# Start and seam of a fused gated mix of linear attention and a SwiGLU FFN: order of the first keys, of the loads, and of the small products

## The chip, the cores and the metric

The kernel runs on one core of one Trainium2 chip. The metric is the device time of one execution in microseconds (us); the time of the kernel before is the median of three runs. A profiled execution gives the trace from which all durations here are read. The engines are PE (TensorE, with PEld for its weight loads), DVE (VectorE), ACT (ScalarE), POOL (GpSimd) and SP (SyncE, which here only issues DMAs).

## The reference

The input x has 2048 tokens of 512 elements, bf16. Two branches read it and a gate per token mixes them:

```python
def reference(A_x, A_wqkv, A_wo, B_x, B_w1, B_w3, B_w2, gate_w):
    def _A_ref(x, wqkv, wo):                      # H = 32 heads of Dh = 16
        ...
        phi = lambda t: jnp.where(t > 0, t + 1, jnp.exp(t)) + 1e-6
        pq, pk = phi(q), phi(k)
        kv = jnp.einsum("bhsd,bhse->bhde", pk, v)
        z = jnp.einsum("bhsd->bhd", pk)
        num = jnp.einsum("bhqd,bhde->bhqe", pq, kv)
        den = jnp.einsum("bhqd,bhd->bhq", pq, z)[..., None] + 1e-6
        o = num / den
        return ... @ wo
    def _B_ref(x, w1, w3, w2):                    # F = 1376
        ...
        h = _silu(gate) * up
        return ...                                # h @ w2
    x = A_x
    g = _sigmoid((x * gate_w).sum(-1, keepdims=True))
    a = _A_ref(x, A_wqkv, A_wo)
    b = _B_ref(x, B_w1, B_w3, B_w2)
    return g * a + (1 - g) * b
```

The attention is linear: kv and z are sums over all tokens, so every token's key must be known before the first output can be formed. The kernel uses kv = pk' (x wv) = (pk' x) wv, so it first accumulates XP = x' pk over the tokens and multiplies by wv once at the end.

## The kernel before, in words

Tokens are cut into 16 tiles of 128 (t = 0 to 15), four tiles make a block of 512 (tb = 0 to 3). The 512 input elements are four chunks (kc, or dc) of 128, since a matmul contracts over 128 partitions. F is 10 chunks of 128 (fc) and a remainder of 96.

**Loads.** DMAs are issued from two queues, each in order: SP's (`dq`, L92) and ACT's. x is wanted twice: with tokens on the partitions (`x_sb`), and transposed (`xT`). For the first block PE transposes x from `x_sb`; for the other three blocks a transposing DMA writes `xT` (L98). ACT's queue issues the four chunks of wk (L95). SP's issues x tile 0, x tiles 1 to 3, then for each later block a transposing load and a plain load (L98, L102), and then wq, the remainder's columns and the gate vector (`wr_sb`), wv, w1, w3, wo, w2.

**Start.** Eight matmuls of zeros (`warm`, L148) and one for a block mask run first. Then comes the key phase: for each tile `emit_k` (L155) transposes x on PE for t under 4 (L160, ACT copies the result out, L164), does four k matmuls (L167), and `phi` (L132) turns k into pk: an exponential on ACT, two operations on DVE. POOL adds pk into `pks`, the sum for z. Two tiles later (`SKEW`) `emit_xp` (L177) adds x' pk to `XP_ps`, four matmuls into four PSUM banks held as one tile. The first two q tiles of block 0 lie between the last XP products, so that PE has work while pk is made. Then ACT and DVE copy XP out in four pieces (L339, L341).

**Seam.** `psO` and `psQ`, the PSUM pools of two banks each that come next, lie where XP_ps was. PE's order is: q tiles 2 and 3, z (`z_ps`, a matmul of ones with pks in float32, L349), the remainder of the FFN for block 0 (`emit_rem`: 96 columns of w1 and w3 and the gate vector), kvT (16 small matmuls of wv with XP_sb, L360, masked to the heads' diagonal blocks by DVE, L364), FFN chunk 0, and W = kvT wo (L371, copied by ACT). `emit_den` (POOL: pq times z, `qz`, L200; DVE: the sum over each head, L203) is emitted for all four tiles right behind the remainder, and `emit_norm` (L251) behind it: 1/den times exp of the gate, POOL's `pqn` (L265), and a transposing DMA from SP into `pqT` (L270).

**Steady part.** For each block: the FFN chunks (`emit_ffn`, L275: four gate and four up matmuls, tanh on ACT, L293, two DVE operations, `gs` L295 and `hT` L298), then for each of its four tiles the next block's q, half of its remainder, the output product `emit_out` (15 matmuls in one PSUM bank, scaled by ACT, stored by SP), and the next block's den; then the next block's norm.

**What sets the order.** PE's order is the order of the program text (`manual_schedule` for PE alone, L143). The order on ACT, DVE, POOL and SP is chosen by the tile framework's scheduler from the emission order and its own cost estimates; each engine then runs its list strictly in that order. [...]

Of the kernel before, what the change touches and what calls it, by code (L numbers as in the profile page):

```python
# [8 lines left out]
ACT = mybir.ActivationFunctionType  # L9
# [3 lines left out]
FP32 = mybir.dt.float32  # L13
BF16 = mybir.dt.bfloat16
# [3 lines left out]
def kernel(  # L18
# [12 lines left out]
    nc = tc.nc  # L31
    P = nc.NUM_PARTITIONS

    Bb, S, D = A_x.shape
# [3 lines left out]
    KC = D // P  # L38
    NT = S // P
# [51 lines left out]
    x_r = x2d.rearrange("(t p) d -> p t d", p=P)  # L91
    dq = nc.sync  # L92
    dq.dma_start(out=x_sb[:, 0:1, :], in_=x_r[:, 0:1, :])
    for kc in range(KC):
        nc.scalar.dma_start(out=wk_sb[:, kc, :], in_=wqkv_r[:, kc, D : 2 * D])  # L95
    dq.dma_start(out=x_sb[:, 1:TPB, :], in_=x_r[:, 1:TPB, :])
    for tb in range(1, NTB):
        dq.dma_start(  # L98
            out=xT[:, :, tb * TB : (tb + 1) * TB], in_=x2d[tb * TB : (tb + 1) * TB, :],
            transpose=True,  # L100
        )
        dq.dma_start(  # L102
            out=x_sb[:, tb * TPB : (tb + 1) * TPB, :], in_=x_r[:, tb * TPB : (tb + 1) * TPB, :]
        )
    dq.dma_start(out=wq_sb[:], in_=wqkv_r[:, :, 0:D])
    dq.dma_start(out=wr_sb[:, :, 0:FR], in_=w1_r[:, :, FM:F])
# [24 lines left out]

    def phi(dst, ps):  # L132
        e = work.tile([P, D], BF16, tag="phi_e", name="phi_e")
        nc.scalar.activation(out=e[:], in_=ps, func=ACT.Exp)  # L134
        em = work.tile([P, D], BF16, tag="phi_m", name="phi_m")
        nc.vector.tensor_scalar(  # L136
            out=em[:], in0=e[:], scalar1=1.0, scalar2=1e-6, op0=ALU.min, op1=ALU.add
        )
        nc.vector.scalar_tensor_tensor(  # L139
            out=dst, in0=ps, scalar=0.0, in1=em[:], op0=ALU.max, op1=ALU.add  # L140
        )

    ctx.enter_context(tc.manual_schedule(engines={ENG.PE}))  # L143


    warm = psM.tile([P, TB], FP32, tag="mm", name="warm")
    for i in range(8):
        nc.tensor.matmul(warm[:], lhsT=zeros[:, 0:P], rhs=zeros[:], start=True, stop=True)  # L148
    mask_ps = psM.tile([P, P], FP32, tag="mm", name="mask_ps")
    nc.tensor.matmul(mask_ps[:], lhsT=EhT[:], rhs=EhT[:], start=True, stop=True)  # L150
# [1 line left out]

    st = {}

    def emit_k(t):  # L155
        ts_tok = slice(t * P, (t + 1) * P)
        if t < TPB:
            xTp = psM.tile([P, KC, P], BF16, tag="mm", name="xTp")
            for kc in range(KC):
                nc.tensor.transpose(  # L160
                    out=xTp[:, kc, :], in_=x_sb[:, t, kc * P : (kc + 1) * P],
                    identity=ident[:],
                )
            nc.scalar.activation(out=xT[:, :, ts_tok], in_=xTp[:], func=ACT.Copy)  # L164
        k_ps = psM.tile([P, D], FP32, tag="mm", name="k_ps")
        for kc in range(KC):
            nc.tensor.matmul(  # L167
                k_ps[:], lhsT=xT[:, kc, ts_tok], rhs=wk_sb[:, kc, :],
                start=(kc == 0), stop=(kc == KC - 1),
            )  # L170
        phi(pk_sb[:, t, :], k_ps[:])
        if t == 0:
            nc.gpsimd.tensor_copy(pks[:], pk_sb[:, t, :])
        else:
            nc.gpsimd.tensor_add(pks[:], pks[:], pk_sb[:, t, :])  # L175

    def emit_xp(t, XP_ps):  # L177
        for dc in range(KC):
            nc.tensor.matmul(  # L179
                XP_ps[:, dc, :], lhsT=x_sb[:, t, dc * P : (dc + 1) * P], rhs=pk_sb[:, t, :],  # L180
                start=(t == 0), stop=(t == NT - 1),
            )

# [14 lines left out]
    def emit_den(tb, tt):  # L198
        qz = work.tile([P, D], FP32, tag="qz", name="qz")
        nc.gpsimd.tensor_tensor(  # L200
            out=qz[:], in0=st[tb, "pq"][:, tt, :], in1=z_sb[:], op=ALU.mult
        )
        nc.vector.tensor_reduce(  # L203
            out=st[tb, "den"][:, tt, :], in_=qz[:].rearrange("p (h d) -> p h d", d=Dh),
            axis=AX.X, op=ALU.add,
        )
# [44 lines left out]
    def emit_norm(tb):  # L251
        rden = blk.tile([P, TPB, H], FP32, tag="rden", name="rden")
        den = st[tb, "den"]
        nc.vector.tensor_scalar(
            out=rden[:], in0=den[:], scalar1=1e-6, scalar2=None, op0=ALU.add
        )
        nc.vector.reciprocal(out=rden[:], in_=rden[:])
        nc.vector.tensor_tensor(  # L258
            out=rden[:], in0=rden[:],
            in1=st[tb, "el"][:, :, None].to_broadcast([P, TPB, H]), op=ALU.mult,  # L260
        )
        pqT = blk.tile([P, KC, TB], BF16, tag="pqT", name="pqT")
        for tt in range(TPB):
            pqn = work.tile([P, D], BF16, tag="pqn", name="pqn")
            nc.gpsimd.tensor_tensor(  # L265
                out=pqn[:].rearrange("p (h d) -> p h d", d=Dh),
                in0=st[tb, "pq"][:, tt, :].rearrange("p (h d) -> p h d", d=Dh),
                in1=rden[:, tt, :, None].to_broadcast([P, H, Dh]), op=ALU.mult,
            )
            nc.sync.dma_start(  # L270
                out=pqT[:, :, tt * P : (tt + 1) * P], in_=pqn[:], transpose=True
            )
        st[tb, "pqT"] = pqT

    def emit_ffn(tb, fc):  # L275
        tok_sl = slice(tb * TB, (tb + 1) * TB)
        fsl = slice(fc * P, (fc + 1) * P)
        if fc == 0:
            st[tb, "hT"] = blk.tile([P, FC, TB], BF16, tag="hT", name="hT")
        gate_ps = psM.tile([P, TB], FP32, tag="mm", name="gate_ps")  # L280
        for kc in range(KC):
            nc.tensor.matmul(  # L282
                gate_ps[:], lhsT=w1_sb[:, kc, fsl], rhs=xT[:, kc, tok_sl],
                start=(kc == 0), stop=(kc == KC - 1),
            )
        up_ps = psM.tile([P, TB], FP32, tag="mm", name="up_ps")
        for kc in range(KC):
            nc.tensor.matmul(  # L288
                up_ps[:], lhsT=w3_sb[:, kc, fsl], rhs=xT[:, kc, tok_sl],
                start=(kc == 0), stop=(kc == KC - 1),  # L290
            )
        th = work.tile([P, TB], BF16, tag="th", name="th")
        nc.scalar.activation(out=th[:], in_=gate_ps[:], func=ACT.Tanh, scale=0.5)  # L293
        gs = work.tile([P, TB], BF16, tag="gs", name="gs")
        nc.vector.scalar_tensor_tensor(  # L295
            out=gs[:], in0=th[:], scalar=1.0, in1=gate_ps[:], op0=ALU.add, op1=ALU.mult
        )
        nc.vector.tensor_tensor(  # L298
            out=st[tb, "hT"][:, fc, :], in0=up_ps[:], in1=gs[:], op=ALU.mult
        )  # L300
# [22 lines left out]
        nc.sync.dma_start(out=out2d[t * P : (t + 1) * P, :], in_=o_out[:])  # L323


    SKEW = 2
    with tc.tile_pool(name="psX", bufs=1, space=bass.MemoryType.PSUM) as psX:
        XP_ps = psX.tile([P, KC, D], FP32, tag="XP", name="XP_ps")
        for t in range(NT):
            emit_k(t)  # L330
            if t >= SKEW:
                emit_xp(t - SKEW, XP_ps)
        emit_q(0, 0, psM, "mm")
        emit_xp(NT - 2, XP_ps)
        emit_q(0, 1, psM, "mm")
        emit_xp(NT - 1, XP_ps)
        for dc in range(KC):
            if dc % 2 == 0:
                nc.scalar.activation(out=XP_sb[:, dc, :], in_=XP_ps[:, dc, :], func=ACT.Copy)  # L339
            else:  # L340
                nc.vector.tensor_copy(out=XP_sb[:, dc, :], in_=XP_ps[:, dc, :])  # L341
# [7 lines left out]
    nc.tensor.matmul(z_ps[:], lhsT=ones_f[:], rhs=pks[:], start=True, stop=True)  # L349
    nc.scalar.activation(out=z_sb[:], in_=z_ps[:], func=ACT.Copy)  # L350
    emit_rem(0, 0, psM, "mm")
    emit_rem(0, 1, psM, "mm")
    for tt in range(TPB):
        emit_den(0, tt)
    emit_norm(0)
    kvT_ps = psQ.tile([P, KC, P], FP32, tag="q", name="kvT_ps")
    for c in range(KC):
        csl = slice(c * P, (c + 1) * P)
# [6 lines left out]
        out=kvT_sb[:], in0=kvT_ps[:],  # L365
        in1=blockmask[:, None, :].to_broadcast([P, KC, P]), op=ALU.mult,
    )
    emit_ffn(0, 0)
    for c in range(KC):
        W_ps = psQ.tile([P, D], FP32, tag="q", name="W_ps")  # L370
        nc.tensor.matmul(W_ps[:], lhsT=kvT_sb[:, c, :], rhs=wo_sb[:, c, :], start=True, stop=True)  # L371
        nc.scalar.activation(out=W_sb[:, c, :], in_=W_ps[:], func=ACT.Copy, scale=2.0)

    for tb in range(NTB):
        for fc in range(1 if tb == 0 else 0, FC):
# [42 lines left out]
```

## Time and profile before

| | |
|---|---|
| median of three runs | 202.17 us (200.95 to 202.47) |
| profiled execution | 200.74 us, of it span 199.0 us |
| mean granted PE clock in the profiled execution | 0.957 |
| busy: PE, DVE, ACT, POOL | 182.3, 119.9, 67.2, 59.2 us |
| matmuls of 512 columns, four of them, full clock | 0.86 us |
| HBM read, written | 8.42 MB, 2.10 MB |

Busy time of PE counts a matmul from its start to its end, and matmuls overlap; what matters is when each group starts. The chain of waits is followed back from the last instruction and shows, in order of time, which engine held the end at each point. The windows give the busy time of each engine, the granted clock and the DMA share in a stretch of time. In the timeline's rows the columns are the start, the length, the engine, the line, the operation, and in brackets the idle time before it with what ended it. A trailing q (SPq, ACTq) means the issue of a DMA, which occupies the queue but not the engine's arithmetic.

### The profile page before, as it was taken

What the parts mean: (1) busy time and instruction counts of PE and PEld (TensorE: products, weight loads), DVE (VectorE), ACT (ScalarE), POOL (GpSimd) and SP (SyncE); (2) the same over time, 40 slices, a digit from 0 to 9 for tenths busy, and PEclk for the clock granted to TensorE, in tenths of its full rate; (3) what the DMA queues carried; (4) which work ended last, traced back from release to release, by engine and by line L of the source; (5) the groups of instructions that cost most, each with busy time, mean ns of one, the idle gap of its engine ahead of it and who ended that gap; (6) DMA issues with size and microseconds to landing.
All of it is one profiled execution on the core that took longest, in us unless ns stands there. A gap on an engine that the chain in (4) does not pass through costs nothing.

```text
span 199.0 us, 2401 instructions
## 1 busy us (share of the span) xinstructions
PE 182.3 (92%) x846; PEld 84.2 (42%) x863; DVE 119.9 (60%) x202; ACT 67.2 (34%) x124; POOL 59.2 (30%) x67
## 2 busy tenths in 40 slices
PE   7268999996939999999999999999999999999993
PEld 2123444442603445454444545444454544444440
DVE  0023488788593778655888765578776567878000
ACT  2132333335433334332333433233333323332121
POOL 4014266751736200333540033354003235500000
PEclk9955999999975999999999999999999999999999
DMA  5999999100002300011040001013100101400011
GB/s 183 153 288 289 292 398 354 55 0 2 2 13 43 79 0 0 13 56 37 30 105 0 3 11 55 21 45 87 25 0 7 59 17 53 98 7 0 26 36 48
DMA packets 28205, 14.88 MB, mean 75 GB/s; under 512 B 19648, under 2 KB 27168, under 8 KB 28192
## 3 DMA queue, kind: packets, MB, share of 16 engines
q1 hardware_dynamic: 27616, 14.20, 26.2%
q10 hardware_dynamic: 576, 0.52, 1.2%
q8 instruction: 7, 0.11, 0.2%
q14 instruction: 6, 0.05, 0.1%
HBM read 8.42 MB, written 2.10 MB: 53 GB/s over the span
## 4 chain that ended last, share of the span: by engine, by line
PE 86%; DMA 4%; DVE 3%; ACT 3%; issue 1%; ACTq 1%; POOL 1%; DVEq 0%
PE gate_ps L282 18%; PE o_ps L315 17%; PE up_ps L288 17%; PE k_ps L167 8%; PE XP_ps L179 7%; PE o_ps L307 7%; PE q_ps L192 6%; DMA wk_sb<-in_A_wqkv_dram 4%; PE r_ps L216 2%; PE o_ps L311 2%; ACT phi_e L134 1%; DVE den L203 1%; PE W_ps L371 1%; ACT xT L164 1%; ACTq L95 1%
## 5 line engine op out<-in xcount | busy, mean ns | idle before, releaser
L282 PE MATMUL gate_ps<-xT,w_sb 128*128 128x512 bf16 x157 | 42.0, 388 | 0.2
L288 PE MATMUL up_ps<-xT,w_sb 128*128 128x512 bf16 x156 | 41.6, 386 | 0.2
L200 POOL TENSOR_TENSOR qz<-pq,z_sb 128x512 f32<-128x512 bf16 x16 | 18.5, 1162 | 74.2 <-DVE pq L139 68.5
L293 ACT ACTIVATE th<-gate_ps 128x512 bf16<-128x512 f32 x40 | 23.9, 597 | 42.2 <-PE gate_ps L282 41.8
L315 PE MATMUL o_ps<-w_sb,hT 128*128 128x512 bf16 x156 | 36.9, 379 | 0.2
L136 DVE TENSOR_SCALAR phi_m<-phi_e 128x512 bf16<-128x512 bf16 x32 | 14.5, 452 | 32.7 <-ACT phi_e L134 32.6
L295 DVE SCALAR_TENSOR_TENSOR gs<-th,gate_ps 128x512 bf16<-128x512 bf16 x40 | 27.4, 686 | 10.6 <-ACT th L293 10.4
L298 DVE TENSOR_TENSOR hT<-up_ps,gs 128x512 bf16<-128x512 f32 x40 | 27.6, 690 | 4.3 <-PE up_ps L288 0.4
L282 PEld LDWEIGHTS <-w_sb 128*128 128x128 bf16 x160 | 15.9, 100 | 19.9 <-issue 2.2
L288 PEld LDWEIGHTS <-w_sb 128*128 128x128 bf16 x160 | 15.9, 99 | 19.5 <-issue 1.1
L167 PE MATMUL k_ps<-wk_sb,xT 128*128 128x512 bf16 x62 | 18.3, 415 | 6.3 <-DMA wk_sb<-in_A_wqkv_dram 3.3
L315 PEld LDWEIGHTS <-hT 128*128 128x128 bf16 x160 | 15.6, 97 | 19.0
L175 POOL TENSOR_TENSOR pks<-pks,pk_sb 128x512 f32<-128x512 f32 x15 | 17.4, 1157 | 14.7 <-DVE pk_sb L139 14.3
L320 ACT ACTIVATE o_out<-o_ps,omg 128x512 bf16<-128x512 f32 x16 | 11.0, 687 | 31.7 <-PE o_ps L315 31.7
L265 POOL TENSOR_TENSOR pqn<-pq,rden 128x512 bf16<-128x512 bf16 x16 | 16.5, 1055 | 13.4 <-DVE rden L258 10.4
L134 ACT ACTIVATE phi_e<-k_ps 128x512 bf16<-128x512 f32 x16 | 9.6, 597 | 23.5 <-PE k_ps L167 21.2
L179 PE MATMUL XP_ps<-pk_sb,x_sb 128*128 128x512 bf16 x63 | 17.3, 396 | 0.1
L203 DVE TENSOR_REDUCE den<-qz 128x32 f32<-128x512 f32 x16 | 10.9, 682 | 10.1 <-POOL qz L200 10.1
L192 PE MATMUL q_ps<-wq_sb,xT 128*128 128x512 bf16 x62 | 16.2, 380 | 0.1
L307 PE MATMUL o_ps<-W_sb,pqT 128*128 128x512 bf16 x63 | 16.2, 379 | 0.0
L134 ACT ACTIVATE phi_e<-q_ps 128x512 bf16<-128x512 f32 x16 | 9.5, 597 | 7.7 <-PE q_ps L192 7.7
L139 DVE SCALAR_TENSOR_TENSOR pq<-q_ps,phi_m 128x512 bf16<-128x512 f32 x16 | 11.1, 691 | 0.5
(55 smaller groups left out, 114.3 us busy)
## 6 DMA issues: line engine op xcount, KB each, us to landing
w_sb<-in_B_w_dram SPq DMA_DIRECT2D x3, 1280.0 KB, 9.4
out_dram<-o_out SPq DMA_DIRECT2D x16, 128.0 KB, 1.7
x_sb<-in_A_x_dram SPq DMA_DIRECT2D x3, 512.0 KB, 4.1
wk_sb<-in_A_wqkv_dram ACTq DMA_DIRECT2D x4, 128.0 KB, 4.3
wq_sb<-in_A_wqkv_dram SPq DMA_DIRECT2D x1, 512.0 KB, 5.0
wv_sb<-in_A_wqkv_dram SPq DMA_DIRECT2D x1, 512.0 KB, 4.6
wo_sb<-in_A_wo_dram SPq DMA_DIRECT2D x1, 512.0 KB, 10.4
x_sb<-in_A_x_dram SPq DMA_DIRECT2D x1, 384.0 KB, 4.2
```

Source lines behind the costliest of these rows:

```text
L134: nc.scalar.activation(out=e[:], in_=ps, func=ACT.Exp)
L167: nc.tensor.matmul(k_ps[:], lhsT=xT[:, kc, ts_tok], rhs=wk_sb[:, kc, :], start=(kc == 0), stop=(kc == KC - 1),)
L179: nc.tensor.matmul(XP_ps[:, dc, :], lhsT=x_sb[:, t, dc * P : (dc + 1) * P], rhs=pk_sb[:, t, :], start=(t == 0), stop=(t == NT - 1),)
L192: nc.tensor.matmul(q_ps[:], lhsT=xT[:, kc, ts_tok], rhs=wq_sb[:, kc, :], start=(kc == 0), stop=(kc == KC - 1),)
L200: nc.gpsimd.tensor_tensor(out=qz[:], in0=st[tb, "pq"][:, tt, :], in1=z_sb[:], op=ALU.mult)
L282: nc.tensor.matmul(gate_ps[:], lhsT=w1_sb[:, kc, fsl], rhs=xT[:, kc, tok_sl], start=(kc == 0), stop=(kc == KC - 1),)
L288: nc.tensor.matmul(up_ps[:], lhsT=w3_sb[:, kc, fsl], rhs=xT[:, kc, tok_sl], start=(kc == 0), stop=(kc == KC - 1),)
L293: nc.scalar.activation(out=th[:], in_=gate_ps[:], func=ACT.Tanh, scale=0.5)
L295: nc.vector.scalar_tensor_tensor(out=gs[:], in0=th[:], scalar=1.0, in1=gate_ps[:], op0=ALU.add, op1=ALU.mult)
L298: nc.vector.tensor_tensor(out=st[tb, "hT"][:, fc, :], in0=up_ps[:], in1=gs[:], op=ALU.mult)
L307: nc.tensor.matmul(o_ps[:], lhsT=st[tb, "pqT"][:, c, tsl], rhs=W_sb[:, c, :], start=(c == 0), stop=False,)
L315: nc.tensor.matmul(o_ps[:], lhsT=st[tb, "hT"][:, fc, tsl], rhs=w2_sb[:, fc, :], start=False, stop=(fc == FC - 1),)
```

## The change

There are four parts.

Loads: x tiles 1 to 3 go to ACT's queue, one DMA each; wk's four chunks go to SP's queue, behind x tile 0 and ahead of the transposing loads, which now follow each other directly. The plain x loads of blocks 1 to 3 leave SP's queue; they are issued from ACT's queue after the exponentials of key tiles 0, 2 and 4.

Start: five warm matmuls instead of eight. The keys of tiles 0 to 3 are accumulated in four PSUM banks of their own (`psE`), chunk of wk by chunk of wk, with the transposes of tiles 2 and 3 in between. DVE instead of ACT copies the transposed x out. XP_ps becomes four tiles of one bank each, and its product runs up to four tiles behind the keys, catching up at tiles 12 and 14.

Seam: PE's order is now q, remainder, kvT, z, then the FFN chunks of block 0, with den of tile fc - 1 behind chunks 1 to 4, the norm behind chunk 5, and W two by two behind chunks 1 and 3.

```diff
     dq.dma_start(out=x_sb[:, 0:1, :], in_=x_r[:, 0:1, :])
+    for t in range(1, TPB):
+        nc.scalar.dma_start(out=x_sb[:, t : t + 1, :], in_=x_r[:, t : t + 1, :])
     for kc in range(KC):
-        nc.scalar.dma_start(out=wk_sb[:, kc, :], in_=wqkv_r[:, kc, D : 2 * D])
-    dq.dma_start(out=x_sb[:, 1:TPB, :], in_=x_r[:, 1:TPB, :])
+        dq.dma_start(out=wk_sb[:, kc, :], in_=wqkv_r[:, kc, D : 2 * D])
     for tb in range(1, NTB):
         dq.dma_start(
             out=xT[:, :, tb * TB : (tb + 1) * TB], in_=x2d[tb * TB : (tb + 1) * TB, :],
             transpose=True,
-        )
-        dq.dma_start(
-            out=x_sb[:, tb * TPB : (tb + 1) * TPB, :], in_=x_r[:, tb * TPB : (tb + 1) * TPB, :]
         )
...
-    for i in range(8):
+    for i in range(5):
         nc.tensor.matmul(warm[:], lhsT=zeros[:, 0:P], rhs=zeros[:], start=True, stop=True)
...
+    def emit_xT(t):
+        xTp = psM.tile([P, KC, P], BF16, tag="mm", name="xTp")
         for kc in range(KC):
+            nc.tensor.transpose(
+                out=xTp[:, kc, :], in_=x_sb[:, t, kc * P : (kc + 1) * P], identity=ident[:]
+            )
+        nc.vector.tensor_copy(out=xT[:, :, t * P : (t + 1) * P], in_=xTp[:])
+
+    def emit_k_mm(k_ps, t, kc):
+        nc.tensor.matmul(
+            k_ps[:], lhsT=xT[:, kc, t * P : (t + 1) * P], rhs=wk_sb[:, kc, :],
+            start=(kc == 0), stop=(kc == KC - 1),
+        )
+
+    def emit_k_phi(k_ps, t):
+        e_ins = phi(pk_sb[:, t, :], k_ps[:])
         if t == 0:
             nc.gpsimd.tensor_copy(pks[:], pk_sb[:, t, :])
         else:
             nc.gpsimd.tensor_add(pks[:], pks[:], pk_sb[:, t, :])
+        tb = t // 2 + 1
+        if t % 2 == 0 and tb < NTB:
+            with tc.issue_after(e_ins.ins):
+                nc.scalar.dma_start(
+                    out=x_sb[:, tb * TPB : (tb + 1) * TPB, :],
+                    in_=x_r[:, tb * TPB : (tb + 1) * TPB, :],
+                )
...
-    SKEW = 2
+    with tc.tile_pool(name="psE", bufs=1, space=bass.MemoryType.PSUM) as psE:
+        k0 = [psE.tile([P, D], FP32, tag=f"k{t}", name=f"k0_{t}") for t in range(TPB)]
+        emit_xT(0)
+        emit_xT(1)
+        emit_k_mm(k0[0], 0, 0)
+        emit_k_mm(k0[1], 1, 0)
+        emit_xT(2)
+        emit_k_mm(k0[0], 0, 1)
+        emit_k_mm(k0[1], 1, 1)
+        emit_k_mm(k0[2], 2, 0)
+        emit_k_mm(k0[2], 2, 1)
+        emit_xT(3)
+        emit_k_mm(k0[0], 0, 2)
+        emit_k_mm(k0[1], 1, 2)
+        emit_k_mm(k0[2], 2, 2)
+        emit_k_mm(k0[3], 3, 0)
+        emit_k_mm(k0[3], 3, 1)
+        emit_k_mm(k0[3], 3, 2)
+        for t in range(TPB):
+            emit_k_mm(k0[t], t, 3)
+            emit_k_phi(k0[t], t)
...
     with tc.tile_pool(name="psX", bufs=1, space=bass.MemoryType.PSUM) as psX:
-        XP_ps = psX.tile([P, KC, D], FP32, tag="XP", name="XP_ps")
-        for t in range(NT):
+        XP_ps = [psX.tile([P, D], FP32, tag=f"XP{dc}", name=f"XP{dc}") for dc in range(KC)]
+        n_xp = 0
+        for t in range(TPB, NT):
             emit_k(t)
-            if t >= SKEW:
-                emit_xp(t - SKEW, XP_ps)
+            for u in range(n_xp, n_xp + (2 if t in (NT - 4, NT - 2) else 1)):
+                emit_xp(u, XP_ps)
+                n_xp = u + 1
...
-    z_ps = psQ.tile([P, D], FP32, tag="q", name="z_ps")
-    nc.tensor.matmul(z_ps[:], lhsT=ones_f[:], rhs=pks[:], start=True, stop=True)
-    nc.scalar.activation(out=z_sb[:], in_=z_ps[:], func=ACT.Copy)
     emit_rem(0, 0, psM, "mm")
     emit_rem(0, 1, psM, "mm")
-    for tt in range(TPB):
-        emit_den(0, tt)
-    emit_norm(0)
     kvT_ps = psQ.tile([P, KC, P], FP32, tag="q", name="kvT_ps")
...
-    emit_ffn(0, 0)
-    for c in range(KC):
-        W_ps = psQ.tile([P, D], FP32, tag="q", name="W_ps")
-        nc.tensor.matmul(W_ps[:], lhsT=kvT_sb[:, c, :], rhs=wo_sb[:, c, :], start=True, stop=True)
-        nc.scalar.activation(out=W_sb[:, c, :], in_=W_ps[:], func=ACT.Copy, scale=2.0)
+    z_ps = psQ.tile([P, D], FP32, tag="q", name="z_ps")
+    nc.tensor.matmul(z_ps[:], lhsT=ones_f[:], rhs=pks[:], start=True, stop=True)
+    nc.scalar.activation(out=z_sb[:], in_=z_ps[:], func=ACT.Copy)
+    for fc in range(FC):
+        emit_ffn(0, fc)
+        if 1 <= fc <= TPB:
+            emit_den(0, fc - 1)
+        if fc == TPB + 1:
+            emit_norm(0)
+        if fc in (1, 3):
+            for c in range(fc - 1, fc + 1):
+                W_ps = psQ.tile([P, D], FP32, tag="q", name="W_ps")
+                nc.tensor.matmul(
+                    W_ps[:], lhsT=kvT_sb[:, c, :], rhs=wo_sb[:, c, :], start=True, stop=True
+                )
+                nc.scalar.activation(out=W_sb[:, c, :], in_=W_ps[:], func=ACT.Copy, scale=2.0)
```

More of the change, by code (lines that the diff above doesn't have):

```diff
@@ L133, in phi @@
         e = work.tile([P, D], BF16, tag="phi_e", name="phi_e")
-        nc.scalar.activation(out=e[:], in_=ps, func=ACT.Exp)
+        e_ins = nc.scalar.activation(out=e[:], in_=ps, func=ACT.Exp)
         em = work.tile([P, D], BF16, tag="phi_m", name="phi_m")
@@ L153 @@
     st = {}
[L155 to L165, printed above, removed]
+    def emit_xT(t):
+        xTp = psM.tile([P, KC, P], BF16, tag="mm", name="xTp")
         for kc in range(KC):
-            nc.tensor.matmul(
-                k_ps[:], lhsT=xT[:, kc, ts_tok], rhs=wk_sb[:, kc, :],
-                start=(kc == 0), stop=(kc == KC - 1),
-            )
-        phi(pk_sb[:, t, :], k_ps[:])
+            nc.tensor.transpose(
+                out=xTp[:, kc, :], in_=x_sb[:, t, kc * P : (kc + 1) * P], identity=ident[:]
+            )
+        nc.vector.tensor_copy(out=xT[:, :, t * P : (t + 1) * P], in_=xTp[:])
[6 more added lines that the diff above has]
+        e_ins = phi(pk_sb[:, t, :], k_ps[:])
         if t == 0:
@@ L175, in emit_k @@
             nc.gpsimd.tensor_add(pks[:], pks[:], pk_sb[:, t, :])
+        tb = t // 2 + 1
[5 more added lines that the diff above has]
+                )
+    def emit_k(t):
+        k_ps = psM.tile([P, D], FP32, tag="mm", name="k_ps")
+        for kc in range(KC):
+            emit_k_mm(k_ps, t, kc)
+        emit_k_phi(k_ps, t)
     def emit_xp(t, XP_ps):
@@ L179, in emit_xp @@
             nc.tensor.matmul(
-                XP_ps[:, dc, :], lhsT=x_sb[:, t, dc * P : (dc + 1) * P], rhs=pk_sb[:, t, :],
+                XP_ps[dc][:], lhsT=x_sb[:, t, dc * P : (dc + 1) * P], rhs=pk_sb[:, t, :],
                 start=(t == 0), stop=(t == NT - 1),
@@ L338 @@
             if dc % 2 == 0:
-                nc.scalar.activation(out=XP_sb[:, dc, :], in_=XP_ps[:, dc, :], func=ACT.Copy)
+                nc.scalar.activation(out=XP_sb[:, dc, :], in_=XP_ps[dc][:], func=ACT.Copy)
             else:
-                nc.vector.tensor_copy(out=XP_sb[:, dc, :], in_=XP_ps[:, dc, :])
+                nc.vector.tensor_copy(out=XP_sb[:, dc, :], in_=XP_ps[dc][:])
     psO = ctx.enter_context(tc.tile_pool(name="psO", bufs=2, space=bass.MemoryType.PSUM))
```

3 lines of the change are left out of this document (2 added, 1 removed).

## The prediction

> **What bounds the kernel now.** I read the page first: the span, the share of TensorE (PE), and the strip of 40 slices (4.975 us each).
>
> ```profile
> span 199.0 us, 2401 instructions
> PE 182.3 (92%) x846; PEld 84.2 (42%) x863; DVE 119.9 (60%) x202; ACT 67.2 (34%) x124; POOL 59.2 (30%) x67
> PE   7268999996939999999999999999999999999993
> PEclk9955999999975999999999999999999999999999
> ```
>
> PE sets the time, and it is short of work or slow in two places only: slices 0 to 3 (the start) and slices 10 to 12 (50 to 65 us, the seam between the last X'P product and the FFN). From slice 13 to the end it is full at full clock, and the change doesn't touch that part. Next I read the chain of waits in order of time (columns: start, length, what), for when each stretch begins.
>
> ```profile
> 2.27 8.13 DMA wk_sb<-in_A_wqkv_dram
> ...
> 15.26 1.89 PE k_ps L167 x4
> ...
> 21.93 0.81 PE k_ps L167 x3
> ...
> 45.19 0.86 PE XP_ps L179 x4
> ...
> 59.97 1.71 PE gate_ps L282 x4
> ...
> 77.48 0.86 PE q_ps L192 x4
> ```
>
> The fourth chunk of wk, issued at 2.27, lands at 10.40, and the chain stands on it. Token tile 4 starts at 21.93. Up to there PE has done 16 k matmuls and 8 XP matmuls; four matmuls of 512 columns take 0.865 at full clock (59.97's row shows the half clock: 1.71 for four), so those 24 are 5.2 us of work in 21.9. XP ends at 45.19 + 0.86 = 46.05; call that T0. FFN block 0 ends at 77.48, T0 + 31.4.
>
> The windows show the clock (columns: window, length, busy time of PE, PEld, DVE, ACT, POOL with counts, granted clock, DMA share, GB/s).
>
> ```profile
> 8.00:10.00 2.00, 0.00 (x0) 0.00 (x0) 0.00 (x0) 0.00 (x0) 0.00 (x0) 0.81 1.27 182
> 18.00:20.00 2.00, 1.31 (x8) 0.55 (x6) 0.80 (x2) 0.60 (x1) 1.02 (x1) 0.63 1.06 370
> 48.00:50.00 2.00, 0.66 (x2) 0.40 (x3) 1.97 (x4) 0.59 (x2) 0.00 (x0) 1.00 0.01 4
> 56.00:58.00 2.00, 0.40 (x1) 0.13 (x2) 2.00 (x6) 0.00 (x0) 0.68 (x2) 0.75 0.08 16
> 62.00:64.00 2.00, 2.00 (x7) 0.72 (x6) 1.27 (x2) 0.31 (x1) 1.03 (x2) 0.54 0.36 80
> ```
>
> With only 0.5 and 1.0 as values, the means place the switches: down at 9.24 and 57.0, up at 19.48 and 63.84. So each idle stretch costs twice: the idle time, and half speed for 10.2 and 6.8 us.
>
> **The start.** Rows of the timeline (start, length, engine, line), then loads with time from issue to landing.
>
> ```profile
> 0.81 1.91 ACTq L95 DMA_DIRECT2D wk_sb<-in_A_wqkv_dram  x4
> 0.81 0.39 SPq L93 DMA_DIRECT2D x_sb<-in_A_x_dram  x1
> 1.26 3.60 PE L148 MATMUL warm<-zeros 128*128 128x512 bf16 x8 [1.26 <-DVE zeros L59]
> 1.73 4.76 SPq L98 DMA_TRANSPOSE xT<-in_A_x_dram  x1
> 5.00 0.61 PE L160 MATMUL xTp<-ident,x_sb 128*128 128x128 bf16 x4
> 11.06 0.60 ACT L134 ACTIVATE phi_e<-k_ps 128x512 bf16<-128x512 f32 x1 [4.82 <-PE k_ps L167]
> 15.66 0.58 SPq L102 DMA_DIRECT2D x_sb<-in_A_x_dram  x1
> ```
> ```profile
> x_sb<-in_A_x_dram SPq DMA_DIRECT2D x1, 128.0 KB, 2.6
> DMA to landing us min/median/max: 2.7/4.3/8.1
> DMA to landing us min/median/max: 5.3/6.6/8.9
> DMA to landing us min/median/max: 4.0/4.1/5.5
> ```
>
> The last three are wk (four loads), the xT transposing loads (three), and the x_sb block loads (three). The first transpose, issued at 1.73, landed at 10.63, just after wk's last chunk (10.40): a load issued behind a transpose on the other queue waited for it.
>
> In the changed kernel SP issues x tile 0, four wk chunks (0.48 each, from 1.20), then the transposes from about 3.1; ACT issues x tiles 1 to 3. Taking 2.7 to 4.3 from issue, wk lands by 3.9 (chunk 0) to 7.0 (chunk 3), tile 3 of x by 6.0. Moving wk past the transposes costs these 1.9 us of SP issue; the three x_sb issues (0.58 each, 1.7) leave SP, so wq and all behind it are issued where they were, nothing gained or lost.
>
> PE: five warm matmuls of 0.43 end at 3.40 (three fewer, 1.3 us), the transposes of tile 0 start at 3.7 and end at 4.3. Their eviction moves from ACT (0.60) to DVE; the nearest DVE row is the 0.68 of L341 below, so 0.65 each: first k matmul at 5.1, second at 5.7. From there 15 k matmuls and 8 transposes follow nearly without a gap, at half clock 15 x 0.43 and twice 0.43, 7.3 us, at full 3.7. When does the clock rise? After warm PE idles in bits of 0.1 to 0.5 us until 5.7; before, the rise at 19.48 came 4.2 us after PE became steady at 15.26. I take 9.2: the last chunks (token tiles 0 to 3) end at 10.5 to 11.1, the first of them between 9.6 (full clock from about 6, the DVE evictions in between) and 11.9 (half clock throughout).
>
> [...]
>
> Now four exponentials and four phi chains come at once, where the kernel before spread them out. XP's four banks are those that k0 filled, so XP of tile 0 cannot finish before the fourth phi is read out. Rows (page):
>
> ```profile
> L136 DVE TENSOR_SCALAR phi_m<-phi_e 128x512 bf16<-128x512 bf16 x32 | 14.5, 452 | 32.7 <-ACT phi_e L134 32.6
> L139 DVE SCALAR_TENSOR_TENSOR pq<-q_ps,phi_m 128x512 bf16<-128x512 f32 x16 | 11.1, 691 | 0.5
> ```
>
> Exp 0.60, then 4 x (0.45 + 0.69) = 4.6 on DVE: 10.5 + 0.6 + 4.6 = 15.7 (14.8 to 17.1). ACT's four Exp and two x_sb issues (4 x 0.60 + 2 x 0.58 = 3.6) fit under that. The new wait is about 3 us of PE, with k of tile 4 (0.86) inside it. That cover also hides the first transpose: issued at 3.1, landing 5.3 to 8.9 later, 8.4 to 12.0. From XP of tile 0 onward there are 11 k, 15 XP and 2 q groups of 0.865, 24.2 us. T0 = 15.7 + 0.2 + 24.2 = 40.1 instead of 46.05: a gain of 6.0 (4.5 to 7.5, the upper end with phi_m at less than its mean). The second and third transpose, 4.8 of issue behind the first and each other (7.9, 12.7), land by 16.8 and 21.6 at the latest; tile 8's k comes at 15.9 + 6 x 0.865 = 21.1, tile 12's at 28. The x_sb blocks, issued at 11, 13 and 15, land 4.0 to 8.1 later, by 19.1 for the first; tile 4's XP comes at 22.0. All are hidden, by 2.9 us at the least.
>
> **The seam.** In the kernel before, z sits in front of the remainder and waits for XP's banks; then kvT, one FFN chunk, and W wait on a DVE queue full of den reductions, the norm and the mask.
>
> ```profile
> 48.52 0.68 DVE L341 CAST XP_sb<-XP_ps 128x512 bf16<-128x512 f32 x1
> 49.34 1.10 PE L349 MATMUL z_ps<-pks,ones_f 128*128 128x512 f32 x2 [1.56 <-DVE XP_sb L341]
> 50.27 1.53 PE L216 MATMUL r_ps<-wr_sb,xT 128*128 128x193 bf16 x16
> 51.64 1.05 PE L360 MATMUL kvT_ps<-XP_sb,wv_sb 128*128 128x128 bf16 x16
> 56.87 0.68 DVE L364 TENSOR_TENSOR kvT_sb<-kvT_ps,blockmask 128x512 bf16<-128x512 f32 x1
> ```
>
> PE work from T0 to the end of FFN block 0 at full clock: two q 1.7, remainder 1.4 (1.53 with its latency), kvT 1.05, z 1.1, four W 0.9, ten chunks of 1.73: 23.4 us, in 31.4. So 8.0 us are idle or slow. Changed order: q and remainder take T0 to +3.1; kvT needs the last eviction, which ended at 49.20, +3.15: no gap. z then runs at +4.2, the first gate at +5.3.
>
> What comes last instead is DVE, whose den and norm now lie between the chunks.
>
> ```profile
> L295 DVE SCALAR_TENSOR_TENSOR gs<-th,gate_ps 128x512 bf16<-128x512 bf16 x40 | 27.4, 686 | 10.6 <-ACT th L293 10.4
> L298 DVE TENSOR_TENSOR hT<-up_ps,gs 128x512 bf16<-128x512 f32 x40 | 27.6, 690 | 4.3 <-PE up_ps L288 0.4
> L203 DVE TENSOR_REDUCE den<-qz 128x32 f32<-128x512 f32 x16 | 10.9, 682 | 10.1 <-POOL qz L200 10.1
> L200 POOL TENSOR_TENSOR qz<-pq,z_sb 128x512 f32<-128x512 bf16 x16 | 18.5, 1162 | 74.2 <-DVE pq L139 68.5
> L257 DVE RECIPROCAL rden<-rden 128x128 f32<-128x128 f32 x1 | 0.9, 939 | 0.0
> pqT<-pqn SPq DMA_TRANSPOSE x16, 2.3
> ```
>
> A chunk is 1.73 on PE and 1.38 on DVE; with a den 2.06, so chunks 1 to 4 put DVE behind by 0.33 each, and the norm follows, 0.94 for its reciprocal and by estimate 0.5 for its two smaller steps. PE can be two chunks ahead (four PSUM buffers). Walking gs and hT through with den behind each: gate of chunk 8 finds its buffer held about 0.4 to 0.6 us. If the norm finds no cover in PE's lead at all, it is 1.4 more, 2 us. I take 1: block 0 ends at T0 + 24.4, a gain of 7.0 (4.5 to 8.0). qz on POOL keeps up (1.16 against 1.73 a chunk). The norm ends about +19.5, pqn (POOL, taken as qz, 1.16) and its transpose (2.3) end about +23; the first out needs it at +25.5: hidden with 2 us to spare.
>
> **The sum.** Start 6.0, seam 7.0, steady part 0: 13.0. The profiled execution took 200.74 (span 199.0 and 1.74 around it): 187.7. The three timed runs were 200.95 to 202.47, so the profiled one is low; with the mean of all four, 201.6, as the base, 188.5.
>
> **The rivals.** Beside the forecast (0.56, 184.5 to 190.5):
> [...]
> Second, DVE becomes the bound of FFN block 0 (0.14): den's reductions are queued ahead of gs and wait for POOL: z at +5.9, four qz of 1.16, so gs of chunk 0 after +10.6 instead of +6.6; a seam gain of 3 to 4, about 192.
> Third, loads bind (0.06): x_sb block 1 on ACT's queue lands only behind all three transposes, as wk's last chunk did behind one: 21.6 + 4.1 = 25.7 against a need at 22.0: 3.7 more, 192.2.
> Fourth, it does nothing (0.03): the order on ACT and DVE is not written by hand, and puts back equal waits; about 200 to 202.
> Fifth, slower (0.04): the x_sb issues on ACT's queue hold ACT until the transfer in front has landed, and Exp 1 to 3 stand behind them. SP once waited so:
>
> ```profile
> SPq L112 <- DMA wq_sb<-in_A_wqkv_dram: 0.9, 1, 0.9
> ```
>
> With h per issue the fourth phi ends at 10.5 + 4 x 0.6 + 2h + 1.1 = 14.0 + 2h; T0 = 38.4 + 2h. [...] Against it: four ACT issues took 1.91 together while their loads took up to 8.1. The later waits are hidden by PSUM buffers.
>
> The run-to-run spread here is about 1%, so 1% is what a measurement can tell from no change. Faster 0.93, same 0.03, slower 0.04. Range: 184.5 to 194.0, from both gains at their best off the profiled execution (185.2, and 0.7 of spread) to both at their worst off the mean (192.6, and 1.4 of spread), which takes in the first three rivals.
>
> **What would show it.** Right: no wait on wk over 1 us; k of tile 4 starting at 10 to 13; a wait of PE on DVE (pk of the first tiles) of some 2 to 4 us before XP of tile 0 ends; last XP at 38.5 to 42; clock 1.0 through the seam; gate of chunk 0 about 5 us after the last XP; q of block 1 about 24.5 after it, and from there 121.5 to the end as before. Wrong: x_sb or xT releasing PE; W or gate waiting on DVE over 3 us in all; ACT held at its x_sb issues; the last part not 121.5.

## The result, and the profile after

The changed kernel takes 195.41 us in the median of four runs (193.72 to 196.16). The kernel before, with one more run beside them, takes 201.56 (200.05 to 202.47). The ratio is 0.969, with a 95% interval of 0.960 to 0.978. The kernel is faster, by 6.2 us in the medians, about half of the 13.0 that was forecast; the time lies above the range. The profiled execution took 193.72, of it span 192.0: 7.0 less than the span of before.

First the page of the changed kernel, its span, PE's share and the strip of slices (now 4.8 us each).

```profile
span 192.0 us, 2397 instructions
PE 175.8 (92%) x843; PEld 82.4 (43%) x860; DVE 118.8 (62%) x206; ACT 64.7 (34%) x120; POOL 59.2 (31%) x67
PE   7910899999999999999999999999999999999990
PEclk9996699999999999999999999999999999999997
```

The seam is closed: from slice 5 on PE is full and the clock stands. The start has a hole, slices 2 and 3, which it didn't have so deep before. The chain of waits gives the borders (start, length, what).

```profile
46.18 0.22 PE XP_218 L190
50.38 0.91 PE z_ps L398 x2
69.49 0.86 PE q_ps L203 x4
186.16 1.47 PE o_ps L326 x6
```

| stretch | before | after | gain | forecast |
|---|---|---|---|---|
| start: up to the end of the last XP product | 46.05 | 46.40 | -0.35 | 6.0 |
| seam: from there to the first q of block 1 | 31.43 | 23.09 | 8.34 | 7.0 |
| from there to the last matmul's end | 118.14 | 118.14 | 0 | 0 |
| last matmul to the end of the span | 3.38 | 4.37 | -0.99 | 0 |

So the seam gave all of the gain and more than was forecast, and the start gave nothing. The timeline of the start in the changed kernel (start, length, engine, line, and in brackets the idle time before with what ended it):

```profile
8.94 0.60 ACT L132 ACTIVATE phi_e<-k_0_141 128x512 bf16<-128x512 f32 x1 [5.44 <-PE k_0_141 L163]
...
11.38 0.51 SPq L104 DMA_DIRECT2D wr_sb<-in_B_w_dram  x1
...
15.53 0.39 ACTq L177 DMA_DIRECT2D x_sb<-in_A_x_dram  x1
15.96 0.60 ACT L132 ACTIVATE phi_e<-k_1_142 128x512 bf16<-128x512 f32 x1 [6.43 <-DMA wr_sb<-in_B_w_dram]
...
19.85 0.61 PE L190 MATMUL XP_215<-pk_sb,x_sb 128*128 128x512 bf16 x1 [9.44 <-DVE pk_sb L137]
```

ACT finishes the first exponential at 9.54. The next item in its list is the issue of the first x block load, and that happens at 15.53. The three exponentials behind it wait for 6 us, DVE's phi chains wait for them, the fourth pk ends at 19.79, and PE, which finished the keys of tile 4 at 10.41, stands for 9.44 us. What ended ACT's wait is the landing of `wr_sb`, the remainder's load of w1, which the x load has nothing to do with. Counted over both queues in the order of the issues in this trace, the x load is the 21st DMA and this load the 13th, eight places before. It stands on SP behind the three transposes and wq, is issued at 11.38 and lands 4.1 later, at 15.51. Two issues on SP waited at the same distance (what waited, for what, us in total, times, longest):

```profile
SPq L99 <- DMA x_sb<-in_A_x_dram: 0.7, 1, 0.7
SPq L111 <- DMA wr_sb<-in_B_w_dram: 0.6, 1, 0.6
```

The first transpose is the 9th DMA and the x load on ACT's queue that it waited for, issued at 0.80, the 1st; w3 is the 22nd and the remainder's load of w3 the 14th. Each was issued as the DMA eight places before it had landed, at 3.79 and 16.02. That the two of a pair share a completion semaphore, as the expectations below have it, is the author's reading; no trace shows it.

The clock then fell too (columns: window, length, busy time of PE, PEld, DVE, ACT, POOL, granted clock, DMA share, GB/s):

```profile
14.00:16.00 2.00, 0.00 (x0) 0.00 (x0) 0.00 (x0) 0.04 (x1) 0.00 (x0) 0.94 0.82 141
20.00:22.00 2.00, 2.00 (x6) 0.63 (x5) 0.99 (x2) 0.00 (x0) 1.84 (x3) 0.50 1.06 392
22.00:24.00 2.00, 1.95 (x8) 0.84 (x8) 0.24 (x1) 0.60 (x1) 0.61 (x1) 0.85 1.05 382
```

Down at 15.8, up at 22.6: PE ran at half speed from 19.85 to 22.6, which is 1.4 us more.

### The profile page after: what moved, and what is told of

Read it like the earlier page. It is cut to its first block, busy times and chain, and to the rows that moved or that the text cites. A ratio compares the mean times of both kernels' runs of the same rounds, so it can differ in the third digit from the quotient of the medians.

```text
span 192.0 us, 2397 instructions
## 1 busy us (share of the span) xinstructions
PE 175.8 (92%) x843; PEld 82.4 (43%) x860; DVE 118.8 (62%) x206; ACT 64.7 (34%) x120; POOL 59.2 (31%) x67
## 4 chain that ended last, share of the span: by engine, by line
PE 87%; SPq 4%; DMA 4%; DVE 2%; issue 1%; ACT 1%; ACTq 0%
PE gate_ps L293 18%; PE o_ps L326 18%; PE up_ps L299 18%; PE q_ps L203 7%; PE o_ps L318 7%; PE k_ps L163 5%; SPq L99 4%; PE r_ps L227 3%; DMA wr_sb<-in_B_w_dram 2%; PE XP_215 L190 2%; PE XP_217 L190 2%; PE o_ps L322 2%; PE XP_218 L190 2%; PE XP_216 L190 2%; DMA x_sb<-in_A_x_dram 2%; DVE pk_sb L137 1%
## 5 line engine op out<-in xcount | busy, mean ns | idle before, releaser
L293 PE MATMUL gate_ps<-xT,w_sb 128*128 128x512 bf16 x157 | 40.9, 379 | 0.3
L299 PE MATMUL up_ps<-xT,w_sb 128*128 128x512 bf16 x156 | 40.5, 379 | 0.1
L134 DVE TENSOR_SCALAR phi_m<-phi_e 128x512 bf16<-128x512 bf16 x32 | 13.9, 434 | 31.1 <-ACT phi_e L132 31.1
L293 PEld LDWEIGHTS <-w_sb 128*128 128x128 bf16 x160 | 15.6, 98 | 19.2 <-issue 0.6
L299 PEld LDWEIGHTS <-w_sb 128*128 128x128 bf16 x160 | 15.6, 98 | 19.0 <-issue 0.2
L190 PE MATMUL XP_215<-pk_sb,x_sb 128*128 128x512 bf16 x16 | 6.3, 394 | 9.5 <-DVE pk_sb L137 9.4
L190 PEld LDWEIGHTS <-x_sb 128*128 128x128 bf16 x64 | 6.3, 100 | 17.6 <-DVE pk_sb L137 9.9
L132 ACT ACTIVATE phi_e<-k_ps 128x512 bf16<-128x512 f32 x12 | 7.2, 599 | 18.1 <-PE k_ps L163 10.8
L163 PE MATMUL k_ps<-wk_sb,xT 128*128 128x512 bf16 x47 | 12.6, 392 | 0.0
## 6 DMA issues: line engine op xcount, KB each, us to landing
x_sb<-in_A_x_dram ACTq DMA_DIRECT2D x3, 512.0 KB, 13.1
```

The costliest lines, as they stand in the source:

```text
L163: nc.tensor.matmul(k_ps[:], lhsT=xT[:, kc, t * P : (t + 1) * P], rhs=wk_sb[:, kc, :], start=(kc == 0), stop=(kc == KC - 1),)
L190: nc.tensor.matmul(XP_ps[dc][:], lhsT=x_sb[:, t, dc * P : (dc + 1) * P], rhs=pk_sb[:, t, :], start=(t == 0), stop=(t == NT - 1),)
L293: nc.tensor.matmul(gate_ps[:], lhsT=w1_sb[:, kc, fsl], rhs=xT[:, kc, tok_sl], start=(kc == 0), stop=(kc == KC - 1),)
L299: nc.tensor.matmul(up_ps[:], lhsT=w3_sb[:, kc, fsl], rhs=xT[:, kc, tok_sl], start=(kc == 0), stop=(kc == KC - 1),)
```

## The experiments

All times in this section are read beside runs of the kernel before on the same chip.

**Each part alone.** The seam of the changed kernel in the kernel before, and the reverse: the changed kernel with the old seam. The edits swap whole sections of text:

```diff
 # seam alone, in the kernel before: from z to W replaced by the changed kernel's text
-    emit_ffn(0, 0)
-    for c in range(KC):
...
+    for fc in range(FC):
+        emit_ffn(0, fc)
+        if 1 <= fc <= TPB:
+            emit_den(0, fc - 1)
...
 # start alone, in the changed kernel: the same section put back
```

> The kernel before with the seam of the changed kernel alone (order of PE, den and norm between the FFN chunks, W two by two); loads and start as before. Theory (all of the measured gain is the seam's): the last XP product at 46 as before, block 0 of the FFN over about 23.3 later instead of 31.4, span 191 to 192, time about 193 to 194.5. Rival (the seam needs XP in four tiles or the changed start): a gain under 6.

> The changed kernel with the seam of the kernel before: loads, keys by chunk, XP in four tiles as changed. Theory (the start gains nothing while ACT is held): last XP product at about 46, the seam 30 to 31.5 long, the span 197.5 to 200, no difference that can be told from before. Rival (start and seam each give about half): 3 us faster.

The seam alone takes 193.40 (191.8 to 194.8) against 199.99, ratio 0.975 (0.967 to 0.982). The start alone takes 200.32, ratio 1.002 (0.998 to 1.006). Chain of waits of the seam alone, then of the start alone:

```profile
43.42 0.86 PE XP_ps L179 x4
...
67.75 0.86 PE q_ps L192 x4
```
```profile
46.38 0.86 PE XP L190 x4
...
76.12 0.86 PE q_ps L203 x4
```

Seam alone: 44.28 to 67.75, 23.5 instead of 31.4. Start alone: the last XP product ends at 47.24, no earlier than before, and its seam, in the old order, is 28.9. That is shorter than the 30 to 31.5 expected, because z no longer waits for XP's copy (1.6 us in the kernel before) and the half speed ended earlier behind W (four gate matmuls took 1.71 and the four up matmuls behind them 1.45, then 0.86 again; in the kernel before 1.71, 1.71 and 1.15). The gain is the seam's. XP in four tiles is not needed for it: the seam alone has XP as one tile.

**The x block loads out of ACT's list.** The three loads go to SP, behind the transposes.

```diff
+    for tb in range(1, NTB):
+        dq.dma_start(
+            out=x_sb[:, tb * TPB : (tb + 1) * TPB, :], in_=x_r[:, tb * TPB : (tb + 1) * TPB, :]
+        )
     dq.dma_start(out=wq_sb[:], in_=wqkv_r[:, :, 0:D])
...
-        if t % 2 == 0 and tb < NTB:
-            with tc.issue_after(e_ins.ins):
-                nc.scalar.dma_start(
...
```

> The changed kernel, but the three plain x loads of blocks 1 to 3 are issued from SP, behind the three transposing loads and ahead of wq; ACT issues only x tiles 1 to 3. Theory (the changed kernel lost the start because its ACT stood for 6.0 us, 9.54 to 15.53, at the first x block load, waiting for a completion semaphore that the remainder's load of w1 still used): with no DMA in ACT's list between the exponentials the four phi chains end at about 13.5 instead of 19.8, the last XP product at about 39 to 40 instead of 46.2, the span falls by 6 to 7.5 to 185 to 186, the time to about 187 to 189. Rival (the wait is that of the loads themselves: PE would next be released by x or by DVE and the start gains less than 3): span 189 or more, and PE released by a DMA.

The profiled execution took 186.12, span 184.3. Its chain of waits, and what PE waited for in all up to 70 us (total, times, longest):

```profile
13.70 0.61 DVE pk_sb L141
14.31 0.04 issue
14.35 1.04 PE XP L187 x4
```
```profile
38.70 0.86 PE XP L187 x4
...
62.66 0.86 PE q_ps L200 x4
```
```profile
PE XP L187 <- DVE pk_sb L141: 3.9, 1, 3.9
PE warm L151 <- DVE zeros L59: 1.3, 1, 1.3
```

The fourth pk ends at 14.31 instead of 19.79, the last XP product at 39.56 instead of 46.40, and the seam is 23.1 as in the changed kernel. These 5.5 us, and the 1.4 of clock that went with them, are what ACT's hold cost, and the numbers are near those of the prediction (fourth phi 15.7, last XP product 40.1). They come from one execution, the fastest of four: the median is 189.76 (186.12 to 190.30) against 199.99 for the kernel before, above the 187 to 189 expected. What is left is the wait that the prediction named, 3.9 us of PE on DVE. The three others took 189.25 to 190.30, with a span of 187.4 to 187.9 and a mean clock of 0.982 instead of 0.997; where they lost it isn't recorded, but 0.015 of 187 is 2.8 us of full clock lost, twice that at half speed, and the only long idle of PE is this one.

**Another predecessor for the same load.** If ACT waits for the DMA eight places before, three DMAs fewer in between must change what it waits for. The gate vector's four loads become one.

```diff
-    gw_r = gate_w.rearrange("(kc d o) -> kc d o", d=P, o=1)
-    for kc in range(KC):
-        dq.dma_start(out=wr_sb[:, kc, 2 * FR : NR], in_=gw_r[kc, :, :])
+    gw_r = gate_w.rearrange("(kc d o) -> d kc o", d=P, o=1)
+    dq.dma_start(out=wr_sb[:, :, 2 * FR : NR], in_=gw_r)
```

> The changed kernel, but the gate vector's four loads are one, so that three DMAs fewer lie between and the load eight before the first x block load is the second transposing load instead of the remainder's load of w1; eight before the second x block load is wq. Theory (ACT waits for the landing of the DMA eight before in the order of both queues): ACT's first x issue ends its wait with the second transpose, at about 10.8 instead of 15.5, the second with wq, at about 15.0; the fourth phi ends at about 17.5 to 18 instead of 19.8 and the span falls by 1.5 to 2.5, to about 190. Rival (ACT's issue is held in hardware while SP's queue is being filled with transposes and loads): the first wait still ends at about 15.5 and the span stays at 192 to 193.5.

The timeline of its start:

```profile
11.41 0.43 ACTq L176 DMA_DIRECT2D x_sb<-in_A_x_dram  x1
11.89 1.09 ACT L131 ACTIVATE phi_e<-k 128x512 bf16<-128x512 f32 x2 [2.35 <-DMA xT<-in_A_x_dram]
...
18.16 0.39 ACTq L176 DMA_DIRECT2D x_sb<-in_A_x_dram  x1
18.65 0.60 ACT L131 ACTIVATE phi_e<-k 128x512 bf16<-128x512 f32 x1 [5.68 <-DMA wq_sb<-in_A_wqkv_dram]
```

Both releasers are the ones named beforehand, a transpose and wq. In the order of the changed kernel, with three DMAs fewer, the two loads are the 18th and the 20th DMA, and eight places before them stand the second transpose and wq. The first hold ends 4.1 us earlier than in the changed kernel. That ACT is held until the DMA eight places before has landed, not while SP's queue is being filled, is shown. The time was missed (196.30 in the one execution there is): wq landed 6.8 after its issue and not 4.2, so the second hold lasted until 18.16 and the fourth pk ended at 20.3; the span is 193.3, where the rival had put it, though not for the rival's reason. Why wq took longer isn't shown; the first x block was issued in the same moment (11.41, wq at 11.37).

**The same loads at another place in ACT's list.** Behind the exponentials of tiles 4, 6 and 8.

```diff
-        tb = t // 2 + 1
-        if t % 2 == 0 and tb < NTB:
+        tb = t // 2 - 1
+        if t % 2 == 0 and 1 <= tb < NTB:
```

> The changed kernel with the x block loads still on ACT, but behind the exponentials of tiles 4, 6 and 8 instead of 0, 2 and 4. Theory (the same wait of about 15.5 for the completion semaphore, but at a place where only the exponential of tile 5 stands behind it): the fourth phi ends at about 13.5, the first XP product at about 15; then the first x block, issued at about 15.5 and landing behind weights (9.7 later in the changed kernel), is late: XP of tile 4 waits for it until about 25 instead of 22, span about 187 to 189. Rival (the place makes no difference, the loads themselves are the bound): 192 to 193.5.

```profile
PE XP L190 <- DVE pk_sb L137: 3.9, 1, 3.9
PE XP L190 <- DMA x_sb<-in_A_x_dram: 1.6, 1, 1.6
```
```profile
16.41 9.10 DMA x_sb<-in_A_x_dram
25.50 0.05 issue
25.55 1.04 PE XP L190 x4
```
```profile
14.43 1.89 PE L190 MATMUL XP<-pk_sb,x_sb 128*128 128x512 bf16 x4 [3.91 <-DVE pk_sb L137]
```

The first issue comes 0.9 later than in the changed kernel (16.41), but the four first exponentials are past it, and PE waits 3.9 for DVE as with the loads on SP. Here this wait did cost the clock: the first XP product took 1.89 instead of 1.04, and the mean clock is 0.982, as in the three other executions with the loads on SP. Then the load itself, behind w1 on the other queue, takes 9.1 us and holds the XP product of tile 4 until 25.55. Span 189.5, just above the 187 to 189 expected, time 191.21, in one execution.

**What is left of the start.** Two edits on top of the loads on SP: the keys of tiles 4 to 7 ahead of the first XP product, and the first four keys finished tile by tile instead of together.

```diff
 # keys ahead: how many XP products follow the keys of tile t (1 where none is given)
+        N_XP = {4: 0, 5: 0, 6: 0, 7: 2, 9: 2, 11: 2, 13: 2, 14: 2}
-            for u in range(n_xp, n_xp + (2 if t in (NT - 4, NT - 2) else 1)):
+            for u in range(n_xp, n_xp + N_XP.get(t, 1)):
...
 # tile order: xT(2) and xT(3) move, the matmuls of tiles 2 and 3 go to the end
...
+        emit_k_mm(k0[0], 0, 3)
+        emit_k_phi(k0[0], 0)
+        emit_k_mm(k0[1], 1, 3)
+        emit_k_phi(k0[1], 1)
+        emit_xT(3)
+        for t in (2, 3):
+            for kc in range(KC):
+                emit_k_mm(k0[t], t, kc)
             emit_k_phi(k0[t], t)
```

> The kernel with the x block loads on SP, and the keys of tiles 4 to 7 all ahead of the first XP product (then XP two by two at tiles 7, 9, 11, 13, 14). Theory (what is left of the start's loss is the wait of the first XP product for the fourth phi, 3.9 us of idle PE, and the clock that falls in some executions because of it): three key tiles, 2.6 us, fill the wait; the first XP product still ends at about 15, the last at about 37, the span is about 182, and the clock stays at 0.99 or more in all executions, so that the times lie within 1% at about 184. Rival (DVE, with eight phi chains in a row, is behind and holds the key phase): PE waits for DVE again at tile 8, span 184 or more.

> The kernel with the x block loads on SP; of the first four keys, tiles 0 and 1 are finished as soon as the last wk chunk lands (about 6.5), then tiles 2 and 3 one after the other, instead of all four chunk by chunk. Theory (with wk landed by 6.5, the order chunk by chunk only makes all four keys end at once, at 8.7 to 9.4, and DVE is idle till then): first exponential at about 7.0 instead of 8.96, first XP product complete about 2 us earlier, span about 182.5. Rival (order chunk by chunk is needed because wk lands late): PE waits for wk over 1 us, and nothing is gained.

> Both: keys of tiles 4 to 7 ahead of XP, and the first four keys tile by tile. Theory: PE finds work from the first transpose on; the span is about 181, 3 us under that with the x block loads on SP, the clock at 0.99 or more in all executions, the time about 183. Rival: DVE is the bound of the start, and the two gains do not add: 182 or more.

| kernel | median (range), us | ratio to before (95%) | spans | first XP product starts |
|---|---|---|---|---|
| keys ahead | 183.84 (183.38 to 185.01) | 0.924 (0.912 to 0.936) | 181.6 to 182.0 | 14.43 |
| tile order | 185.05 (184.56 to 186.65) | 0.930 (0.919 to 0.940) | 182.7 to 184.8 | 13.20 |
| both | 183.29 (182.60 to 184.00) | 0.920 (0.910 to 0.929) | 180.3 to 182.2 | 14.86 |
| both, once more | 182.53 (182.28 to 184.03) | 0.916 (0.910 to 0.922) | 180.2 to 182.2 | 12.83 |

What PE waited for, keys ahead and then tile order:

```profile
PE XP L187 <- DVE pk_sb L141: 1.3, 1, 1.3
```
```profile
PE XP L187 <- DVE pk_sb L141: 2.5, 1, 2.5
```

Three key tiles fill 2.6 of the 3.9, and with them the mean clock is 1.0 in all four executions and their spans lie within 0.4 us. Tile by tile the keys start DVE earlier, though by 1.1 and not 2 (DVE's list has the copy of x tile 3 ahead of the first phi), and in the profiled execution the clock still fell in the wait:

```profile
12.00:14.00 2.00, 0.81 (x3) 0.36 (x4) 1.73 (x4) 0.00 (x0) 1.84 (x3) 0.87 0.95 256
14.00:16.00 2.00, 2.00 (x6) 0.69 (x5) 0.00 (x0) 0.00 (x0) 1.92 (x2) 0.50 1.08 373
```

With both, PE waits for nothing longer than 0.3 us between the first matmul and the end of the FFN's first block. The first profiled execution of both had the clock up late, at about 9.5 (four key matmuls took 1.71 at 7.62, and eight 1.73 at 9.68; the slow ones moved XP to 14.86), the second had it up by 5.75 (0.59 for two key matmuls, then 0.86 for four). This first rise is read from the matmuls: the granted clock reads 1.00 in the windows from 0 to 4 us of the kernel before, the changed kernel and the second execution of both, though the warm matmuls follow each other at 0.43 us, as at half speed, so the mean clock doesn't contain it. The page of the second:

```profile
span 180.2 us, 2417 instructions
PE 175.1 (97%) x860; PEld 82.3 (46%) x860; DVE 119.2 (66%) x206; ACT 64.9 (36%) x120; POOL 59.6 (33%) x67
```

This version beats both kernels: its ratio to the kernel before is 0.916 where the changed kernel's is 0.969.

**Warm matmuls.** The version with both, with eight warm matmuls again instead of five.

```diff
-    for i in range(5):
+    for i in range(8):
```

> The kernel with both changes of the start once more, beside the next one on the same chip: 182.5 to 184.

> The same with eight warm matmuls instead of five, as in the kernel before. The first transpose then starts at 5.0 instead of 3.7, 1.3 us later. [...] Rival (the clock does not matter there, PE waits for wk and DVE anyway): 1.3 us slower, 184.5.

182.98 (182.70 to 183.30), ratio 0.916 (0.911 to 0.922), against 182.53 for five: the difference can't be told from none. The first XP product starts at 13.86 against 12.83 in the profiled executions, so a good start is 1.0 us later with eight, and the spread of the six times is 0.6 us against 1.75. The rival seems to hold in part: eight warm matmuls cost 1.0 where five are enough, near its 1.3, though the median is not at its 184.5. They may also make the start more even, which rests on six times each, of which the one at 184.03 makes the wider spread; its clock at the start isn't recorded.

## Why the prediction was right or wrong

**The step that failed** is the sentence "ACT's four Exp and two x_sb issues (4 x 0.60 + 2 x 0.58 = 3.6) fit under that". An issue was costed at the length of its row. What it waits for before it issues was not asked of these three loads, and the first one waited 6.0 us. That an issue occupies only the queue holds for the length of its row alone (the issue at 16.20, 0.38 long, and the exponential at 16.45 overlap): the exponentials behind the first issue in ACT's list waited with it, from 9.54 to 15.96. The fourth phi came out at 19.8 instead of 15.7, the last XP product at 46.4 instead of 40.1, with 1.4 us of it the clock. Taken out of ACT's list, the loads leave 14.3 and 39.6, and a start 6.5 shorter than before against 6.0 forecast. That the rest of the start's sum came so close is in part luck, since two errors offset each other: the fourth phi ended 1.4 earlier than summed, and the sum left 0.2 for XP of tile 0 behind it, where all four of its matmuls (1.04) came behind it.

**The rival that happened** is the fifth, with a chance of 0.04, in a smaller size: "the x_sb issues on ACT's queue hold ACT until the transfer in front has landed". Its formula, with one h of 6.0 instead of two, gives 20.0 for the fourth phi, measured 19.8. This agreement is luck too: the first exponential came 1.6 earlier than in the formula, and behind the hold DVE's three phi chains took 3.2 where it had 1.1 for one. Its mechanism was off: not the transfer in front on ACT's queue, but the DMA eight places before over both queues. The row beside it, "SPq L112 <- DMA wq_sb", was this very wait: w1 is the 21st DMA of the kernel before and wq the 13th. It was read as a queue that waits for its last transfer, and the evidence against it, "four ACT issues took 1.91 together", came from four of the first eight DMAs, which have none eight places before them.

**The seam** was right in its mechanism and sized at 7.0 against 8.3 measured (8.0 in the seam alone). The 1 us allowed for DVE wasn't lost: PE went from the last XP product to block 1 in 23.1, the 23.4 of work that was summed. The second rival, den ahead of gs, did happen in the order of DVE's list (den of tile 0 at 53.26, gs of chunk 0 at 53.87, 1.1 us after its tanh had ended) and PE, by then in the second chunk (its up matmuls at 53.72), had no wait in the block.

**The clock**, which had a chance of 0.17, did fall at the start, as a consequence of the hold, and cost 1.4 us. How much work of PE keeps it up isn't shown: the window from 10 to 12 us held 0.41 us of it and the one from 12 to 14 none, and the clock read 1.00 in both. **The third**, loads that bind, didn't in the changed kernel; with the issue moved behind tile 4's exponential it did, at 9.1 us from issue to landing. The instance it started from, that wk's last chunk had waited for a transpose in the kernel before, isn't what the trace shows, though it landed only at 10.40: from 5 to 10 us ACT's queue, which held wk alone, moved 11 to 54 packets in each us, beside 322 to 621 of SP's.

**Smaller terms.** DVE's eviction of transposed x took 0.42, not 0.65. The clock was up before the second half of the first keys (a k matmul took 0.61 at 4.85 and 0.38 at 5.83), not at 9.2, so the last chunks ended at 8.9 to 9.6 and not 10.5 to 11.1; in one execution of the version with both it was up only at 9.5. With the two the first exponential came 1.6 us earlier than predicted. The phi chains came to 4.7 for four as summed. wk landed by 6.5, within the sum. SP's later issues did not stay where they were: wq was issued at 10.76 instead of 16.29.

**The steady part** took 118.14 in both. The end took 1.0 us longer in the profiled execution of the changed kernel, 0.8 of it the landing of the last store (2.5 instead of 1.7), which nothing here explains.

## What to carry to other kernels

A DMA issued from an engine that also computes is an item in that engine's list, and what it waits for holds the items behind it. Here ACT's exponentials stood for 6.0 us at an issue of 0.39, until the DMA eight places before it, counted over both queues, had landed; look up which earlier DMA ends such a wait before costing the issue at its length. When a wait in the profile is ended by a transfer that the waiting instruction doesn't read, suspect a wait of this kind: the six such rows read here (wr_sb, xT and wq_sb on ACT, wq_sb on SP in the kernel before, x_sb and wr_sb on SP in the changed one) all lie eight places apart. And work that is brought together at one point moves the load onto the engine behind it: four keys at once were 4.7 us of phi chains on DVE, and PE waited for 3.9 of them; fill the wait with work that needs only what is there. In the four executions with the keys ahead the clock then stayed up as well (a mean of 1.0).

## What the runs showed of the hardware that was not expected

Three transposing loads issued one straight behind the other took less time than the same loads with plain loads between and beside them. In the kernel before an issue took 3.2 to 4.8 and the landing 5.3 to 8.9; in the changed kernel an issue took 2.0 to 2.5 and the landing 4.4 to 4.8, the longest of them the first:

```profile
xT<-in_A_x_dram SPq DMA_TRANSPOSE x1, 4.8
```

The runs don't separate the order from the absence of traffic on the other queue.

Two queues that had loads open together moved nearly as many packets each, not as many bytes. The x blocks, 512 KB each, were issued on ACT's queue at 15.5 to 17.0 while SP's queue held the weights, and took 9.7, 13.1 and 16.6 us to land, at a total rate of 380 to 392 GB/s in the windows from 18 to 26 us; 512 KB is 1.3 to 1.4 us at that rate. Before 18 none of their packets had moved. From 20 to 26 each window of 2 us held nearly as many packets of ACT's queue (219 to 221) as of SP's (215 to 225), but ACT's hold 1 KB and SP's 2.5 KB on the mean, so ACT's queue got 0.21 to 0.22 of 0.76 to 0.78 MB. With the same loads on SP ahead of the weights the longest took 6.5.

In the changed kernel the clock fell only at 15.8, after 5.4 us without a matmul. The wait of 3.9 us left the clock up in the profiled execution with the x loads on SP (mean clock 0.997, first XP product 1.04) and lowered it in the run with the loads behind tile 4's exponential (0.982, 1.89), though the first exponential and the first XP product lie at the same times to 0.1 us (8.96 and 9.04, 14.35 and 14.43). What decides between the two isn't shown.
